# Decode attention over two key/value caches: the small cache and each head of the large one as loop bodies with fixed buffers

## The chip, the core, the metric

The kernel runs on one core of a Trainium2 chip. The metric is device time in microseconds (us). All runs quoted here are fast (granted clock 0.83 to 0.85), and a kernel's time is the median of its runs, unless "span" is said: the span is that of the one profiled execution, which is shorter than the time of the same run.

## The reference, cut to what matters

One token is decoded against two caches. Problem A (the "large cache") has 32 heads with their own keys and values; problem B (the "small cache") has 8 key/value heads, each shared by 4 query heads, and looks at the last 4096 keys only.

```python
# A: x [1,1,512], k_cache and v_cache [1, 32, 32768, 128] bf16, wq [512, 4096], wo [4096, 512]
q = (x @ wq).reshape(B, Sq, 32, 128).transpose(0, 2, 1, 3)
scores = einsum("bhqd,bhkd->bhqk", q, k_cache) * 128 ** -0.5
o = einsum("bhqk,bhkd->bhqd", softmax(scores), v_cache)
out_A = o.transpose(0, 2, 1, 3).reshape(B, Sq, 4096) @ wo
# B: the same with k_cache and v_cache [1, 8, 32768, 128]; k, v = last 4096 keys, each head repeated 4 times
return concatenate([out_A, out_B], axis=-1)
```

One head of A has 8.39 MB of keys and as many values; the used part of B has 8.39 MB of keys and 8.39 MB of values in all. Every byte is used once, so this is a stream from memory with a little arithmetic hung on it.

## The kernel before

Loads are issued by SyncE in program order on one queue, and they come in in that order (the four loads issued in the first 3 us of the trace, 4.19 MB each, have landed at about 13, 24, 34 and 44 us). `kbuf` has three parts ("thirds") of 32 KB per partition, `vbuf` has two. A large head's keys take two thirds, its values all of `vbuf`.

The names in the code: `qproj` is the query projection; `unit` the transposes of a group's or head's keys and the score matmuls; `stats` the maximum and the exponential of the scores; `PT` the transposes of the exponentials and `PV` their product with the values; `spread` what closes a cache. A score matmul is 32 columns wide (`128*32` in the profile's lines, where a transpose has `128*128`); its place, a column strip, is set by `tile_position`, and it writes 32 partitions.

```python
    def load_b(self, which, g):                # small cache: group g (4 heads) has its own third / half
        w = HALF * DH
        dst = {"k": self.kbuf, "v": self.vbuf}[which][:, w * g:w * g + w].rearrange("p (s x) -> p s x", s=4)
        self.load(dst, self.kv_src(which, "B", g), self.mark(which, g), self.free[which][g])
        # kv_src: "s (p j) d -> p s (j d)", p=128: 8 KB runs

    def k_thirds(self, g):
        return (1, 0) if g % 2 == 0 else (1, 2)

    def load_v(self, g):                       # large cache: waits until both halves of vbuf are free
        self.load(self.vbuf[:, :], self.kv_src("v", "A", g)[:, 0, :], self.mark("v", 0), *self.free["v"])

    # plan(), the order of the work
        self.load_wq("B")                      # into half 0 of vbuf
        self.load_b("k", 0)
        self.load_wq("A")                      # into half 1 of vbuf
        self.load_b("k", 1)
        self.emit_qproj("B")
        self.emit_unit("B", 0)
        self.emit_qproj("A")                   # frees half 1 of vbuf
        self.emit_stats("B", 0)
        self.emit_unit("B", 1, {1: lambda: self.emit_PT("B", 0)})
        self.emit_stats("B", 1)
        for g in range(2):
            if g == 1:
                self.emit_PT("B", g)
            self.load_b("v", g)
            self.emit_PV("B", g)
        self.emit_spread("B")
        for g in range(NQH):
            self.loop = {"pe": g // 2, "dve": g // 2}     # two heads per iteration
            self.load_k(g, 1 if g < NQH - 1 else 2)
            self.load_v(g)
            self.emit_qcopy(g)
            self.emit_unit("A", g)             # transposes of the keys and score matmuls
            self.emit_stats("A", g)
            self.emit_PT("A", g)
            self.emit_PV("A", g)

    # a batch: 8 transposes into PSUM, one copy to kt; then the scores, four column strips at a time
    def emit_S(self, key):
        # ... (win: the 32 columns that hold the query in its place)
                for c in range(STRIPS):
                    inst = e.matmul(self.S[32 * c:32 * c + 32, :], lhsT=win,
                                    rhs=self.kt[(bb + c // 2) % NKT][:, 512 * (c % 2):512 * (c % 2) + 512],
                                    start=begin, stop=end, tile_position=(0, 32 * c), skip_group_check=True)
```

Of the kernel before, what the change touches and what calls it, by code (L numbers as in the profile page):

```python
# [35 lines left out]
class Op:  # L36
# [5 lines left out]
    __slots__ = ("eng", "fn", "deps", "loop", "pos", "to", "users", "before")  # L42

    def __init__(self, eng, fn, deps, to, loop):
        self.eng = eng
        self.fn = fn
        self.deps = [d for d in deps if d is not None]
        self.to = to
        self.loop = loop
        self.users = []  # L50


class _Kernel:

    def __init__(self, nc, a, b, out):
# [27 lines left out]
        self.loop = {}  # L83



    def op(self, eng, fn, *deps, to=None):
        o = Op(eng, fn, deps, to, self.loop.get(eng))
        self.prog[eng].append(o)
        return o  # L90
# [15 lines left out]
    def assign(self, eng):  # L106


        ops = self.prog[eng]
        pos, last = 0, None  # L110
        for o in ops:
            pos = pos + 1 if o.loop is not None and o.loop == last else 0
            o.pos, last = pos, o.loop
# [43 lines left out]
    def emit(self, eng):  # L157
        ops = self.prog[eng]
        nit = len({o.loop for o in ops} - {None})
        its = [[o for o in ops if o.loop == k] for k in range(nit)]  # L160
        first = next((i for i, o in enumerate(ops) if o.loop is not None), len(ops))
        pre, post = ops[:first], ops[first + sum(map(len, its)):]
# [17 lines left out]
        def body(e):  # L180
            seen, base = {}, {}
            straight(e, pre, seen, base)
            if not nit:
                return

# [5 lines left out]
            for name in [x for x in sems if not step[x]]:  # L191
                if top(0, name) > seen.get(name, 0):
                    e.wait_ge(sems[name], top(0, name))
                    seen[name] = top(0, name)
                del sems[name]
# [18 lines left out]
            for name, sem in sems.items():  # L214
                if start[name] > 0:
                    e.sem_inc(sem, -start[name])._wait_ge(sem, start[name])
                elif start[name] < 0:
                    e.sem_inc(sem, -start[name])
            with e.Fori(0, nit):
                for o, w in zip(its[-1], plans[-1]):  # L220
                    run(e, o, [(sems[name], rel) for name, rel in w])
                for name, sem in sems.items():
                    e.sem_inc(sem, -step[name])._wait_ge(sem, step[name])
            for name in sems:
                base[name] = seen[name] = start[name] + step[name] * nit
            straight(e, post, seen, base)
# [3 lines left out]
    def alloc(self):  # L230
# [4 lines left out]
        self.kt = [sb(f"kt{i}", [128, 1024], BF16) for i in range(NKT)]  # L235
# [13 lines left out]
        for name, d in self.X.items():  # L249
# [3 lines left out]
                oc=[sb(f"oc_{name}{i}", [128, DH + 1], F32) for i in range(2)],  # L253
# [3 lines left out]
                nb=sb(f"nb_{name}", [128, 2], F32),  # L257
# [9 lines left out]
        self.qa = sb("qa", [128, NQH], BF16)  # L267
        self.qw = sb("qw", [128, 64], BF16)
# [8 lines left out]
        self.ksem = [s(f"ksem{i}") for i in range(2)]  # L277
        self.vsem = [s(f"vsem{i}") for i in range(2)]
# [22 lines left out]
    def load_b(self, which, g):  # L301

        w = HALF * DH
        dst = {"k": self.kbuf, "v": self.vbuf}[which][:, w * g:w * g + w].rearrange("p (s x) -> p s x", s=4)
        self.load(dst, self.kv_src(which, "B", g), self.mark(which, g), self.free[which][g])
# [44 lines left out]
    def plan(self):  # L350
# [12 lines left out]
        self.load_b("k", 0)  # L363
        self.load_wq("A")
        self.load_b("k", 1)
        self.emit_qproj("B")
        self.emit_unit("B", 0)
        self.emit_qproj("A")
        self.emit_stats("B", 0)
        self.emit_unit("B", 1, {1: lambda: self.emit_PT("B", 0)})  # L370
        self.emit_stats("B", 1)
        for g in range(2):
            if g == 1:
                self.emit_PT("B", g)
            self.load_b("v", g)
            self.emit_PV("B", g)
        self.emit_spread("B")

        for g in range(NQH):
            self.loop = {"pe": g // 2, "dve": g // 2}  # L380
            self.load_k(g, 1 if g < NQH - 1 else 2)
            self.load_v(g)
            self.emit_qcopy(g)
            self.emit_unit("A", g)
# [12 lines left out]
    def constants(self):  # L397
# [8 lines left out]
        pool(lambda g: g.memset(self.qw[:, :], 0.0))  # L406
        pool(lambda g: g.memset(self.spread[:, :, :], 0.0))
        pool(lambda g: g.memset(self.rows64[:, :], 0.0))
        pool(lambda g: g.memset(self.nscale[:, :], -self.SCALE))
        for n in ("B", "A"):  # L410
            pool(lambda g, n=n: g.memset(c[n]["hsel"][:, :], 0.0))
# [27 lines left out]
    def emit_qproj(self, name):  # L439
        t = self.c[name]  # L440
        slot = self.WQ_SLOT[name]
        ps, wq = self.ACC, self.vbuf[:, HALF * DH * slot:HALF * DH * (slot + 1)]
        def mm(e):
            inst = None
            for tt in range(4):
                for h in range(NQH):
                    inst = e.matmul(ps[:, h:h + 1], lhsT=wq[:, 4096 * tt + 128 * h:4096 * tt + 128 * h + 128],
                                    rhs=t["x"][:, tt:tt + 1], start=(tt == 0 and h == 0), stop=(tt == 3),
                                    skip_group_check=True)
            return inst  # L450
        o = self.op("pe", mm, (self.xsem[name], 16), self.landed("v", slot), self.accread, to="dve")
        self.free["v"][slot] = o
        if name == "B":
            o = self.op("dve", lambda v: v.tensor_copy(
                self.qz[:, 32:].rearrange("p (k w) -> p k w", w=32)[:, 0:8, 0:4],
                ps[:, 0:NQH].rearrange("p (k a) -> p k a", a=4)), o, self.k_pool)
            self.qb = o
        else:
            o = self.op("dve", lambda v: v.tensor_copy(self.qa[:, :], ps[:, 0:NQH]), o)
            self.qready = o  # L460
        self.accread = o

    def emit_qcopy(self, g):
        self.qcopy = self.op("act", lambda s: s.activation(
            out=self.qw[:, 32:33], in_=self.qa[:, g:g + 1], func=ACTF.Copy), self.qready, self.k_hw, to="pe")

    def emit_unit(self, name, g, hooks={}):

        d = self.X[name]
        thirds = (g,) if name == "B" else self.k_thirds(g)  # L470
        lo = min(thirds)
        order = [(t, i, 8 * (t - lo) + st) for i, t in enumerate(thirds) for st in range(8)]
        for n, (t, i, st) in enumerate(order):
            for half in range(2):
                self.emit_T(HALF * lo + 16 * st + 8 * half, self.landed("k", g if name == "B" else i), t)
            if n % 2:
                if n // 2 in hooks:
                    hooks[n // 2]()
                self.pending.append((name, g, order[n - 1][2], n == 1, n == len(order) - 1, self.nbatch - 4))
                if len(self.pending) > 1:  # L480
                    self.emit_S(self.pending.pop(0))

    def emit_T(self, tile, landed, third):
# [3 lines left out]
        src = self.kbuf[:, DH * tile:DH * tile + 1024]  # L487
        def tr(e):
            inst = None
            for k in range(8):  # L490
                inst = e.transpose(T[:, 128 * k:128 * k + 128], src[:, DH * k:DH * k + DH], self.ident[:, :])  # L491
            return inst
        o = self.op("pe", tr, landed, self.copies[b - NT] if b >= NT else self.k_ident, to="dve")
        self.copies.append(self.op("dve", lambda v: v.tensor_copy(KT[:, :], T[:, :]), o, to="pe"))  # L494
        self.free["k"][third] = o

    def emit_S(self, key):
        name, g, st0, first, last, b0 = key
        d = self.X[name]
        for st in (st0, st0 + 1):  # L500
            s, kc = divmod(st, d["KC"])
            row = kc * d["HG"] + s * d["rep"]
            if name == "A":
                win = self.qw[:, 32 - row:64 - row]
            else:
                off = 32 + 32 * (g * d["kvg"] + s) - row
                win = self.qz[:, off:off + 32]
            bb = b0 + 2 * (st - st0)
            begin, end = first and st == st0, last and st > st0
            def mm(e, win=win, bb=bb, begin=begin, end=end):  # L510
                inst = None
                for c in range(STRIPS):
# [4 lines left out]
            o = self.op("pe", mm, self.qcopy if name == "A" else self.qb, self.copies[bb + 1],  # L517
                        self.sread if first else None, to="dve" if end else None)
        self.sdone = o

    def emit_stats(self, name, g):

        self.emit_S(self.pending.pop(0))
# [3 lines left out]
        k = g % 2  # L527
# [4 lines left out]
        if name == "A":  # L532
# [7 lines left out]
            o = dve(lambda v: v.tensor_copy(t["nb"][:, k:k + 1], self.ACC[:, 64:65]), o, to="act")  # L540
            self.sread = self.op("act", lambda s: s.activation(  # L541
                out=self.psb[:, :], in_=self.S[:, :], func=ACTF.Exp, bias=t["nb"][:, k:k + 1], scale=self.SCALE,
                accum_out=t["oc"][k][:, DH:DH + 1]), o, self.psread, to="pe")
# [5 lines left out]
        for c in range(STRIPS):  # L549
# [4 lines left out]
        o = dve(lambda v: v.tensor_scalar_mul(t["nb"][:, k:k + 1], t["cm"][:, 0:1], -self.SCALE), o, to="act")  # L554
        self.sread = self.op("act", lambda s: s.activation(
            out=self.psb[:, :], in_=self.S[:, :], func=ACTF.Exp, bias=t["nb"][:, k:k + 1], scale=self.SCALE,
            accum_out=t["oc"][k][:, DH:DH + 1]), o, self.psread, to="pe")

    def emit_PT(self, name, g):
        d, t = self.X[name], self.c[name]  # L560
        PT = self.PT[:, :].bitcast(BF16)
        def pt(e):
            inst = None
            for jj in range(4):
                inst = e.transpose(PT[:, 128 * jj:128 * jj + 128], self.psb[:, 128 * jj:128 * jj + 128], self.ident[:, :])  # L565
# [4 lines left out]
        if name == "A":  # L570
            self.hcopy = self.op("act", lambda s: s.activation(
                out=self.hw[:, :], in_=t["hsel"][:, 32 - g:64 - g], func=ACTF.Copy), self.k_sel, to="pe")

    def emit_PV(self, name, g):
# [8 lines left out]
        else:  # L583
            w = HALF * DH
            vv = self.vbuf[:, w * g:w * g + w].rearrange("p (s t x) -> p s t x", s=4, x=DH)
# [10 lines left out]
        pv = self.op("pe", mm, self.landed("v", 0 if name == "A" else g), self.ptread, self.accread, to="sp")  # L596
# [107 lines left out]
```

## Time and profile before

| | before |
|---|---|
| time, median of 4 runs | 1328.89 us (1328.62 to 1329.13) |
| span of the profiled run | 1326.8 us |
| bytes loaded | 570.43 MB, 430 GB/s over the span |
| TensorE waits for large keys | 164.4 us, 31 times |
| first large V load issued | 67.61 us |

From the page of the kernel before: what the DMA engines moved in 40 equal slices of the span, and the load queue (q1) and an instruction queue (q8; the page doesn't name its engine, the author took it as TensorE's, since no other engine has so long a program) with packets, MB and their share of 16 engines.

```profile
GB/s 394 431 431 438 432 433 433 437 429 433 433 435 437 433 435 431 433 433 435 437 433 435 431 433 433 431 441 433 431 435 433 431 433 441 433 431 435 433 431 344
...
q1 hardware_dynamic: 12776, 570.43, 99.6%
q8 instruction: 12, 0.20, 0.1%
```

The row is flat: between the first and the last slice nothing falls under 429 GB/s. The packets of the load queue fill 99.6% of the time of the 16 DMA engines, so this stream is what bounds the kernel.

From the timeline of the kernel before, 54 to 135 us: start, length, engine and line, what, and in brackets how long the engine had been idle and what ended it. SPq is SyncE issuing a load.

```profile
54.63 0.34 SPq L286 DMA_DIRECT2D kbuf<-in_A_k_cache_dram  x1
...
67.61 0.34 SPq L286 DMA_DIRECT2D vbuf<-in_A_v_cache_dram  x1
...
83.45 5.79 PE L491 MATMUL psT<-ident,kbuf 128*128 128x128 bf16 x64 [12.95 <-DMA kbuf<-in_A_k_cache_dram]
...
94.49 0.33 SPq L286 DMA_DIRECT2D kbuf<-in_A_k_cache_dram  x1
...
115.97 0.33 SPq L286 DMA_DIRECT2D vbuf<-in_A_v_cache_dram  x1
```

The first large K load is issued at 54.63 and has landed at 83.45, where TensorE starts on it. The first large V load was issued at 67.61, so it stood in the queue 16 us before its turn.

From the windows of the kernel before: each stretch with its length, the busy time of PE (TensorE's matmuls), its weight loads, DVE, ACT and POOL, the granted clock, the DMA share and, in the last column, GB/s. Over a few us the last two are rough, and shares above 1 occur.

```profile
42.00:46.00 4.00, 1.84 (x18) 1.84 (x19) 1.86 (x8) 0.78 (x2) 0.00 (x0) 0.50 1.00 412
...
80.00:86.00 6.00, 2.55 (x25) 2.55 (x26) 1.31 (x2) 0.00 (x0) 0.00 (x0) 0.50 0.98 426
86.00:90.00 4.00, 4.00 (x55) 3.47 (x54) 3.52 (x7) 0.00 (x0) 0.00 (x0) 0.78 0.95 410
90.00:96.00 6.00, 6.00 (x104) 4.95 (x101) 6.00 (x11) 0.00 (x0) 0.00 (x0) 1.00 1.18 505
```

### The profile page before, as it was taken

What the parts mean: (1) busy time and instruction counts of PE and PEld (TensorE: products, weight loads), DVE (VectorE), ACT (ScalarE), POOL (GpSimd) and SP (SyncE); (2) the same over time, 40 slices, a digit from 0 to 9 for tenths busy, and PEclk for the clock granted to TensorE, in tenths of its full rate; (3) what the DMA queues carried; (4) which work ended last, traced back from release to release, by engine and by line L of the source; (5) the groups of instructions that cost most, each with busy time, mean ns of one, the idle gap of its engine ahead of it and who ended that gap; (6) DMA issues with size and microseconds to landing.
All of it is one profiled execution on the core that took longest, in us unless ns stands there. A gap on an engine that the chain in (4) does not pass through costs nothing.

```text
span 1326.8 us, 28797 instructions
## 1 busy us (share of the span) xinstructions
PE 964.5 (73%) x13436; PEld 679.5 (51%) x13436; DVE 749.8 (57%) x1345; ACT 54.8 (4%) x167; POOL 2.3 (0%) x17
## 2 busy tenths in 40 slices
PE   3757678777667877766787777678777767877786
PEld 3544455554445555444565544456554445655453
DVE  3645466665456666545666645566654556665473
ACT  0000000000000000000000000000000000000000
POOL 0000000000000000000000000000000000000000
PEclk9877788887788888778888878888887888888798
DMA  9999999999999999999999999999999999999998
GB/s 394 431 431 438 432 433 433 437 429 433 433 435 437 433 435 431 433 433 435 437 433 435 431 433 433 431 441 433 431 435 433 431 433 441 433 431 435 433 431 344
DMA packets 13079, 570.66 MB, mean 430 GB/s; under 512 B 1540, under 2 KB 1544, under 8 KB 1928
## 3 DMA queue, kind: packets, MB, share of 16 engines
q1 hardware_dynamic: 12776, 570.43, 99.6%
q8 instruction: 12, 0.20, 0.1%
q10 hardware_dynamic: 288, 0.00, 0.0%
q14 instruction: 3, 0.02, 0.0%
HBM read 570.43 MB, written 0.00 MB: 430 GB/s over the span
## 4 chain that ended last, share of the span: by engine, by line
DMA 70%; PE 28%; DVE 1%; issue 0%; SPq 0%; ACT 0%
DMA kbuf<-in_A_k_cache_dram 65%; PE psT L491 23%; PE psS L513 4%; DMA kbuf<-in_B_k_cache_dram 3%; DMA kbuf<-in_A_wo_dram 3%; DVE kt L494 1%; PE psACC L593 0%; SPq L286 0%; DVE oc_A L609 0%; ACT psb L541 0%; DVE tr_in L530 0%; PE psPT L565 0%; ACT ptsb L568 0%; PE psPT L655 0%; PE psG L620 0%
## 5 line engine op out<-in xcount | busy, mean ns | idle before, releaser
L494 DVE COPY kt<-psT 128x1024 bf16<-128x1024 bf16 x1056 | 655.2, 684 | 245.0 <-PE psT L491 243.1
L491 PE MATMUL psT<-ident,kbuf 128*128 128x128 bf16 x8448 | 579.2, 234 | 176.2 <-DMA kbuf<-in_A_k_cache_dram 164.4
L491 PEld LDWEIGHTS psT<-ident,kbuf 128*128 128x128 bf16 x8448 | 539.7, 106 | 268.2 <-DMA kbuf<-in_A_k_cache_dram 172.5
L593 PE MATMUL psACC<-vbuf,ptsb 128*4 128x512 bf16 (+1 forms) x2112 | 183.2, 523 | 23.1 <-ACT ptsb L568 21.3
L513 PE MATMUL psS<-kt,qw 128*32 128x512 bf16 x2048 | 157.6, 385 | 15.5 <-DVE kt L494 15.5
L607 DVE TENSOR_SCALAR oc_A<-psACC,hot_A 128x128 f32<-128x128 f32 x32 | 11.2, 351 | 247.8 <-PE psG L620 247.8
L593 PEld LDWEIGHTS psACC<-vbuf,ptsb 128*4 128x4 bf16 (+1 forms) x2112 | 60.0, 110 | 136.9 <-issue 87.2
L541 ACT ACTIVATE psb<-psS,nb_A 128x512 bf16<-128x512 f32 x32 | 22.0, 687 | 1169.9 <-DVE nb_A L540 1169.9
L513 PEld LDWEIGHTS psS<-kt,qw 128*32 128x32 bf16 x2048 | 34.0, 95 | 58.0 <-DVE kt L494 31.4
L620 PE MATMUL psG<-oc_A,hw 128*32 128x128 f32 (+1 forms) x128 | 19.3, 227 | 52.3 <-DVE oc_A L609 52.3
L620 PEld LDWEIGHTS psG<-oc_A,hw 128*32 128x32 f32 x128 | 11.4, 109 | 62.4 <-DVE oc_A L609 55.0
L565 PE MATMUL psPT<-ident,psb 128*128 128x128 bf16 x136 | 17.9, 274 | 34.0 <-ACT psb L541 34.0
L609 DVE SCALAR_TENSOR_TENSOR oc_A<-psACC,hot_A,oc_A 128x128 f32<-128x128 f32 x96 | 33.7, 351 | 3.4
L530 DVE TENSOR_REDUCE tr_in<-psS 128x1 f32<-128x512 f32 x34 | 23.5, 692 | 17.1 <-PE psS L513 17.1
L565 PEld LDWEIGHTS psPT<-ident,psb 128*128 128x128 bf16 x136 | 10.0, 116 | 37.0 <-ACT psb L541 36.7
L534 PE MATMUL psACC<-rows,tr_in 128*1 128x64 f32 x64 | 8.7, 217 | 25.6 <-DVE tr_in L530 25.6
L568 ACT ACTIVATE ptsb<-psPT 128x512 bf16<-128x512 bf16 x34 | 20.3, 597 | 28.2 <-PE psPT L565 28.2
L534 PEld LDWEIGHTS psACC<-rows,tr_in 128*1 128x1 f32 x64 | 2.7, 81 | 35.1 <-DVE tr_in L530 35.1
L538 PE MATMUL psACC<-mr_A,nscale 1*128 1x1 f32 x64 | 12.1, 256 | 9.8 <-DVE mr_A L537 9.8
L538 PEld LDWEIGHTS psACC<-mr_A,nscale 1*128 1x128 f32 x64 | 9.4, 183 | 15.7 <-DVE mr_A L537 15.7
L540 DVE COPY nb_A<-psACC 128x1 f32<-128x1 f32 x32 | 5.1, 158 | 15.0 <-PE psACC L538 15.0
L537 DVE TENSOR_REDUCE mr_A<-psACC 1x1 f32<-1x64 f32 x32 | 6.8, 213 | 11.7 <-PE psACC L534 11.7
(71 smaller groups left out, 75.1 us busy)
## 6 DMA issues: line engine op xcount, KB each, us to landing
kbuf<-in_B_k_cache_dram SPq DMA_DIRECT2D x2, 4096.0 KB, 32.5
vbuf<-in_B_v_cache_dram SPq DMA_DIRECT2D x2, 4096.0 KB, 23.6
kbuf<-in_A_k_cache_dram SPq DMA_DIRECT2D x2, 4096.0 KB, 22.0
vbuf<-in_B_wq_dram SPq DMA_DIRECT2D x1, 4096.0 KB, 12.3
vbuf<-in_A_wq_dram SPq DMA_DIRECT2D x1, 4096.0 KB, 32.4
kbuf<-in_B_wo_dram SPq DMA_DIRECT2D x2, 2048.0 KB, 33.1
kbuf<-in_A_wo_dram SPq DMA_DIRECT2D x1, 1408.0 KB, 28.5
kbuf<-in_A_wo_dram SPq DMA_DIRECT2D x1, 1024.0 KB, 30.6
```

The source lines that it names most:

```text
L491: inst = e.transpose(T[:, 128 * k:128 * k + 128], src[:, DH * k:DH * k + DH], self.ident[:, :])
L494: self.copies.append(self.op("dve", lambda v: v.tensor_copy(KT[:, :], T[:, :]), o, to="pe"))
L513: inst = e.matmul(self.S[32 * c:32 * c + 32, :], lhsT=win, rhs=self.kt[(bb + c // 2) % NKT][:, 512 * (c % 2):512 * (c % 2) + 512], start=b ...
L530: o = dve(lambda v: v.reduce_max(tr["in"][:, 0:1], self.S[:, :], axis=AXX), self.sdone, self.k_pool, to="pe" if name == "A" else None)
L534: o = self.op("pe", lambda e: e.matmul(self.ACC[0:1, 0:64], lhsT=tr["in"][:, 0:1], rhs=self.rows64[:, :], start=True, stop=True, skip_grou ...
L538: o = self.op("pe", lambda e: e.matmul(self.ACC[:, 64:65], lhsT=self.nscale[:, :], rhs=t["mr"][0:1, :], start=True, stop=True, skip_group_ ...
L541: self.sread = self.op("act", lambda s: s.activation(out=self.psb[:, :], in_=self.S[:, :], func=ACTF.Exp, bias=t["nb"][:, k:k + 1], scale= ...
L565: inst = e.transpose(PT[:, 128 * jj:128 * jj + 128], self.psb[:, 128 * jj:128 * jj + 128], self.ident[:, :])
L568: self.ptread = self.op("act", lambda s: s.activation(out=self.ptsb[:, :], in_=PT[:, 0:512], func=ACTF.Copy), self.psread, to="pe")
L593: inst = e.matmul(acc[32 * c:32 * c + rows, 0:512], lhsT=lhsT, rhs=rhs, start=begin, stop=end, tile_position=(0, 32 * c), skip_group_check ...
L609: o = self.op("dve", lambda v, src=src, hot=hot: v.scalar_tensor_tensor(out=oc, in0=src, scalar=hot, in1=oc, op0=ALU.mult, op1=ALU.add), p ...
L620: return self.op("pe", lambda e: e.matmul(self.G[0:32, c0 + c:c0 + c2], lhsT=win, rhs=t["oc"][g % 2][:, c:c2], start=False, stop=True, ski ...
```

## The change

Its intent is a smaller program. The small cache becomes a TensorE loop over two groups of heads, and the large cache a loop over single heads instead of pairs; for this the buffers are fixed, so that each pass uses the same addresses. Where the two passes of a pair differ, an if/else picks the side. The small cache's keys are loaded in 32 KB runs: each of the 128 partitions holds 128 neighbouring keys of one head (partition 4b+s: block b, head s). After the transposes the four heads are interleaved, so a score matmul for one head has to pick its columns out of the transposed keys. The core of the diff, with cuts:

```diff
+        kt = [sb(f"kt{i}", [128, 2048], BF16) for i in range(NKT // 2)]
+        self.ktp = [x[:, :].rearrange("p (m i b s) -> p m b i s", m=4, i=4, s=4) for x in kt]
 ...
+    def load_bk(self, g):
+        d = self.X["B"]
+        src = d["k"][0, 4 * g:4 * g + 4, d["key0"]:d["key0"] + d["NKEYS"], :].rearrange("s (b j) d -> b s (j d)", b=32)
         w = HALF * DH
+        self.load(self.kbuf[:, 2 * w:3 * w], src, self.kbsem, self.free["k"][2])
 ...
         self.load_wq("B")
-        self.load_b("k", 0)
+        self.load_bk(0)
         self.load_wq("A")
-        self.load_b("k", 1)
         self.emit_qproj("B")
-        self.emit_unit("B", 0)
+        self.load_bv(0)
+        for g in range(2):
+            self.loop = {"pe": ("b", g)}
+            self.emit_qcopy("B", g)
+            self.emit_unit_b(g)
+            self.emit_stats("B", g)
+            self.emit_PT("B", g)
+            self.emit_PV("B", g)
+            if g == 0:
+                self.load_bk(1)
+                self.load_bv(1)
+        self.loop = {}
+        self.emit_spread("B")
         self.emit_qproj("A")
 ...
         for g in range(NQH):
-            self.loop = {"pe": g // 2, "dve": g // 2}
+            self.loop = {"pe": ("a", g), "dve": ("a", g)}
 ...
+    def emit_Sb(self, step, b0):
+            for s in range(4):
+                for x in range(2):
+                    kc, c = divmod(2 * step + x, 4)
+                    row = 16 * kc + 4 * s
+                    inst = e.matmul(self.S[32 * c:32 * c + 32, :], lhsT=self.qzw[:, 32 + 32 * s - row:64 + 32 * s - row],
+                                    rhs=self.ktp[(b0 // 2 + x) % (NKT // 2)][:, :, :, :, s], start=(kc == 0 and s == 0),
+                                    stop=(kc == 1 and s == 3), tile_position=(0, 32 * c), skip_group_check=True)
 ...
+                        with e.If_eq(odd, 0):          # second half of a large head: its third is 0 or 2
+                            for o, _, w in ops:
+                                run(e, o, [(sems[name], rel) for name, rel in w])
+                        with e.Else():
```

The query projection is also rewritten: rows of 512 on four column strips, then turned, instead of 128 matmuls with one column each. The projection for the large cache now comes after the small cache.

## The prediction

> **What bounds the kernel now.** The DMA engines. The page counts 570.43 MB on the load queue in a span of 1326.8 us, 430 GB/s, and 429 to 441 GB/s in every slice but the first and last (394, 344). The chain of waits gives DMA 70%, PE 28%; PE stands there where a load was issued early and queued behind another. In the timeline the large cache's key loads are issued every 38.2 us (94.49, 132.65); 16.78 MB (one head's K and V) at 433 GB/s take 38.7 us: the queue never runs dry. PE needs 34.6 us for head 0 (83.45 to 118.0); the waits view shows it idle for keys 164.4 us over 31 heads, 5.3 us each. So compute has 4 to 5 us of slack per head, and only DMA idle time or DMA rate moves the span.
>
> **What the change does, costed.**
> 1. Bytes: the same. The small cache's keys (8.4 MB) go from 8 KB to 32 KB runs. The windows show about 418 GB/s from 32 to 56 us, where 8 KB runs flow, against 433 later: 20.1 against 19.4 us, a gain of 0.7 us on the DMA chain.
> 2. The small cache is serialised: both key groups share one buffer. The second key load waits for the first group's transposes (done near 39 us); wq_A and the first V load keep the queue fed to 44 us, so no gap. Its keys land near 53.5 instead of 44.1 us, and the second PV ends near 75 instead of 67.6 us.
> 3. The query projection of the large cache moves from 36 us to behind the small cache. It frees the half of the value buffer that the first large V load needs. From the old durations (S to exp 3.4 us, exp to PV 5, PV to spread 6.4, then about 3.5 for a projection at the lower clock there) I put that load's issue near 82 us, against 67.6. The first large K load, issued near 49, lands near 82.8. [...] a hole of 1 to 4 us opens in the DMA stream near 82 us and is never regained: estimate +2.5 us.
> 4. Large-cache loop: one head per iteration on PE and DVE, with an if/else for the second half of the transposes. [...] In this trace the PE loop ran 16 times while its instruction queue (q8) moved 12 packets, 0.20 MB: the body was not refetched. The new body is shorter, so I expect under 1 us per head, hidden by the key wait. First passes may stall some us once.
> 5. Single oc and nb buffers: reused a head later; no wait.
>
> **Sum.** 1328.7 - 0.7 + 2.5: 1330.5 us, range 1326.5 to 1337. Faster by over 2%: 1%; within 2%: 95%; slower: 4%.
>
> **What would show the steps.** Windows: 430 GB/s or more in the middle slices, one dip near 80 to 86 us. DMA: fewer packets (by about 768). Waits: SP's wait for the first large V load ends on the projection near 82 us. PE's key wait stays over 3 us per head, q8 near 12 packets.
>
> **What would make it wrong.** If branches and back edge cost over 5 us per head [...], PE becomes the bound and each further us per head costs 32 us. If the projection frees the value buffer before 80 us there is no hole, and the time falls slightly below before.

"The lower clock there" is a granted clock of 0.56, 0.59 and 0.84 in the windows 60 to 64, 64 to 68 and 68 to 72 us of the kernel before, and the stall that step 4 allows a first pass was 3.42 us, once, in the change.

## More of the kernel before

The program is recorded as a list of operations per engine with their dependencies, and then emitted; an operation signals one other engine when it is done.

Matmuls on different strips overlapped: in the kernel before, eight on four strips took 0.61 us, where one took 0.38.

From the view of one tile, the score tile `psS`, 20 to 60 us: durations in ns, least, median and most, of the small cache's 64 score matmuls.

```profile
L513 PE MATMUL psS<-kt,qz x64: 378/384/391, 30.6 to 55.5; 128*32 128x512 bf16 x64
```

## The result, and the profile after

| | before | after |
|---|---|---|
| time, median of 4 runs | 1328.89 us | 1343.42 us (1341.05 to 1344.27) |
| span of the profiled run | 1326.8 us | 1341.1 us |
| bytes loaded, GB/s over the span | 570.43 MB, 430 | 570.43 MB, 425 |
| TensorE waits for large keys | 164.4 us, 31 times | 146.0 us, 30 times |
| first large V load issued | 67.61 us | 95.26 us |

The ratio is 1.0106, with a 95% interval of 1.0093 to 1.0119. Ratios here are the mean time of one kernel's fast runs over that of the other's of the same rounds, so they are not quite the ratio of the medians. The change is slower by 14.5 us, inside the 2% band and outside the predicted range.

From the page after: the DMA rate by slices, and the two queues.

```profile
GB/s 394 341 329 432 438 434 418 438 434 434 438 436 434 420 438 436 430 438 436 436 424 434 438 430 436 436 436 426 432 438 430 436 434 436 430 430 438 432 434 354
...
q1 hardware_dynamic: 12008, 570.43, 98.6%
q8 instruction: 7, 0.11, 0.0%
```

The whole loss stands in two of 40 slices, the second and the third, 33 to 101 us. From there on the rate is that of before. The two slices lack some 90 and 102 GB/s against 431; a slice is 33.5 us, so (90 + 102) / 431 x 33.5 = 14.9 us. That is the difference.

From the timeline after, 28 to 108 us.

```profile
29.02 3.72 PE L535 MATMUL psS<-kt,qzw 128*32 128x512 bf16 x8
...
45.43 0.58 SPq L309 DMA_DIRECT2D kbuf<-in_B_k_cache_dram  x1
...
55.73 0.51 SPq L309 DMA_DIRECT2D kbuf<-in_A_k_cache_dram  x1
...
58.72 5.26 PE L564 MATMUL psT<-ident,kbuf 128*128 128x128 bf16 x64 [1.38 <-DMA kbuf<-in_B_k_cache_dram]
...
95.26 0.34 SPq L309 DMA_DIRECT2D vbuf<-in_A_v_cache_dram  x1
...
96.31 5.22 PE L564 MATMUL psT<-ident,kbuf 128*128 128x128 bf16 x64 [0.22 <-PEq L212]
```

The windows after, the same stretches.

```profile
42.00:46.00 4.00, 4.00 (x16) 0.51 (x12) 0.43 (x1) 0.00 (x0) 0.00 (x0) 1.00 0.02 8
...
80.00:86.00 6.00, 1.13 (x14) 0.53 (x16) 2.99 (x13) 1.60 (x5) 0.00 (x0) 0.70 1.08 470
86.00:90.00 4.00, 3.17 (x34) 1.18 (x26) 0.71 (x3) 0.00 (x0) 0.00 (x0) 0.60 0.04 16
90.00:96.00 6.00, 4.00 (x46) 1.66 (x46) 2.76 (x7) 0.00 (x0) 0.00 (x0) 0.72 0.01 3
```

There are two holes in the stream: one of about 4 us from 42 us, and one of about 10 us from 86 us, which ends with the issue of the first large V load. Between them they hold most of the loss. And the score tile after, 20 to 82 us:

```profile
L535 PE MATMUL psS<-kt,qzw x64: 1052/1061/1137, 29.0 to 79.0; 128*32 128x512 bf16 x64
```

The small cache's score matmuls take 1061 ns each instead of 384, and a block of eight takes 3.72 us. No term of the prediction has these matmuls at a new duration. TensorE, which had time to spare in this stage before, is now busy from 23 us to 46 us with the first group alone.

From the waits of SyncE (the DMA queue's own), 0 to 100 us: what it waited for, us in total, times, longest.

```profile
SPq L309 <- PE psS L496: 53.9, 2, 38.9
SPq L309 <- PE psS L535: 27.4, 1, 27.4
```

L496 is the projection, L535 are the slow matmuls. The V load was released by the projection, as predicted, but 13 us later than predicted. The second small key load (45.43) was released by a score matmul and not by the last transposes, which were over at 41.71 us: in this program an operation signals only one other engine, and the transposes signal VectorE.

### The profile page after: what moved, and what is told of

Same layout as the page of the kernel before. It is cut to its first block, busy times and chain, and to the rows that moved or that the text cites. A ratio compares the mean times of both kernels' runs of the same rounds, so it can differ in the third digit from the quotient of the medians.

```text
span 1341.1 us, 28761 instructions
## 1 busy us (share of the span) xinstructions
PE 991.8 (74%) x13260; PEld 682.9 (51%) x13260; DVE 754.1 (56%) x1349; ACT 56.2 (4%) x173; POOL 2.6 (0%) x20
## 3 DMA queue, kind: packets, MB, share of 16 engines
q1 hardware_dynamic: 12008, 570.43, 98.6%
HBM read 570.43 MB, written 0.00 MB: 425 GB/s over the span
## 5 line engine op out<-in xcount | busy, mean ns | idle before, releaser
L564 PE MATMUL psT<-ident,kbuf 128*128 128x128 bf16 x8448 | 584.1, 235 | 153.1 <-DMA kbuf<-in_A_k_cache_dram 146.0
L662 PE MATMUL psACC<-vbuf,ptsb 128*4 128x512 bf16 (+1 forms) x2112 | 186.1, 529 | 23.4 <-ACT ptsb L637 23.4
L535 PE MATMUL psS<-kt,qzw 128*32 128x512 bf16 x64 | 24.6, 1068 | 0.0
L637 ACT ACTIVATE ptsb<-psPT 128x512 bf16<-128x512 bf16 x34 | 20.3, 597 | 21.3 <-PE psPT L634 21.3
```

The costliest lines, as they stand in the source:

```text
L535: inst = e.matmul(self.S[32 * c:32 * c + 32, :], lhsT=self.qzw[:, 32 + 32 * s - row:64 + 32 * s - row], rhs=self.ktp[(b0 // 2 + x) % (NKT ...
L564: inst = e.transpose(T[:, 128 * k:128 * k + 128], self.kbuf[:, DH * tile:DH * tile + DH], self.ident[:, :])
L637: self.ptread = self.op("act", lambda s: s.activation(out=self.ptsb[:, :], in_=PT[:, 0:512], func=ACTF.Copy), self.psread, to="pe")
L662: inst = e.matmul(acc[32 * c:32 * c + rows, 0:512], lhsT=lhsT, rhs=rhs, start=begin, stop=end, tile_position=(0, 32 * c), skip_group_check ...
```

## The experiments

The theory: the score matmuls are slow because they read the transposed keys at a step of 256 bytes (the index `i` runs fastest in `ktp`, and its step is 128 elements of 2 bytes). They lengthen the chain from the second small key load to the end of the small cache; the first large V load hangs on that end; until it is issued the queue has nothing more to do. The rivals: the loop and its branches (L); the shared key buffer and the late projection, whatever the matmuls cost (B); the number of column strips, two instead of four; a loss in the first hole by itself.

The first four runs shared one chip and one set of runs of the kernel before (1328.98 us).

### s8: the step from 256 to 8 bytes

```diff
-        self.ktp = [x[:, :].rearrange("p (m i b s) -> p m b i s", m=4, i=4, s=4) for x in kt]
+        self.ktp = [x[:, :].rearrange("p (m i b s) -> p m i b s", m=4, i=4, s=4) for x in kt]
 ...     # small cache only: the exponential puts its columns back into the order that V has
-                out=self.psb[:, :], in_=self.S[:, :], func=ACTF.Exp, ...
+                out=self.psb[:, :].rearrange("p (m b i) -> p m i b", m=4, i=4), in_=self.S[:, :], func=ACTF.Exp, ...
```

> The changed kernel with one thing different: the small cache's score matmuls read the transposed keys at a step of 4 elements (8 bytes) instead of 128 elements (256 bytes); the exponential writes its columns back into the old order, so the result stays right. Theory S (the far-apart reads slow these matmuls, which delays the end of the small cache and with it the first large V load): a block of 8 score matmuls falls from 3.7 us to about 0.9 us, the second small key load is issued near 38.5 us instead of 45.4, the first large V load near 80 us instead of 95.3, and the time falls to 1328 to 1330.5 us. Rival B (shared buffer and late projection alone, whatever the matmuls cost): the V load stays after 88 us, time above 1336. Rival L (loop and branch of the large cache): no change, 1341 to 1344.

Measured: 1333.83 us (1333.78 to 1334.45), ratio to before 1.0038. 9.6 of the 14.5 us are gone with one index order. From the tile view and the timeline of this run:

```profile
L535 PE MATMUL psS<-kt,qzw x64: 608/629/632, 28.2 to 69.2; 128*32 128x512 bf16 x64
```

```profile
28.23 1.97 PE L535 MATMUL psS<-kt,qzw 128*32 128x512 bf16 x8
...
37.81 0.58 SPq L309 DMA_DIRECT2D kbuf<-in_B_k_cache_dram  x1
...
86.47 0.34 SPq L309 DMA_DIRECT2D vbuf<-in_A_v_cache_dram  x1
```

The expectation was too hopeful: the 8 byte step was not free (629 ns for one matmul, against 379 in the next run). A block takes 1.97 us, not 0.9, and the V load comes at 86.47, not 80. The direction holds and rival L falls; the rest of the loss is larger than expected. A small part of that rest is the repair: the exponential that writes its columns back into order took 1392 ns, against 688 in the change.

### contig: contiguous reads, wrong result

```diff
-                                    rhs=self.ktp[(b0 // 2 + x) % (NKT // 2)][:, :, :, :, s], ...
+                                    rhs=self.kt[(b0 + 2 * x + s // 2) % NKT][:, 512 * (s % 2):512 * (s % 2) + 512], ...
```

> Wrong result on purpose: the small cache's score matmuls read contiguous 512 element pieces. Theory S: as the run with the 8 byte step within 0.5 us if 8 bytes is near enough to be free; if any step costs, this one is faster than that one and a block of 8 takes visibly less. Rival L: no change, 1341 to 1344.

Measured: 1330.66 us (1330.27 to 1331.33), ratio 1.0012 (0.9996 to 1.0029).

```profile
L535 PE MATMUL psS<-kt,qzw x64: 379/379/390, 29.3 to 67.6; 128*32 128x512 bf16 x64
```

A block takes 1.04 us, and the V load is issued at 83.19 us. So the three steps give 379, 629 and 1061 ns for one matmul. In a block of eight on two strips four follow one another, so the block less one record, divided by three, gives an estimate of what one costs when they follow closely: (1.04 - 0.38) / 3 = 0.22 us, (1.97 - 0.63) / 3 = 0.45 us, (3.72 - 1.06) / 3 = 0.89 us. By it the 8 byte step doubled the cost and the 256 byte step made it four times as long; no run shows why a step costs. The step is not all of it: the run bstride below also reads at 256 bytes, but eight elements before it jumps back where the change reads four, and one matmul takes 1284 ns there. No run separates the step from the length of these runs.

With contiguous reads the changed kernel is 1.7 us above before by the medians (the interval allows no difference), close to the +1.8 of the prediction's sum. That closeness is partly luck: the sum has a gain of 0.7 us for the longer runs, which no time shows, and this run still has two strips, on which a contiguous block takes 1.04 us instead of 0.6. But the bulk of what the prediction left out, 12.8 of 14.5 us, goes with the pattern of this read.

This run and the other ones that mix up keys passed the comparison with the reference. So the comparison doesn't see the order of keys, presumably because scores this small make a nearly flat softmax; that the run with 8 bytes is right rests on its index order, not on the comparison.

### strips4: the 256 byte step on four strips, wrong result

```diff
-                    inst = e.matmul(self.S[32 * c:32 * c + 32, :], ...
-                                    ... start=(kc == 0 and s == 0), stop=(kc == 1 and s == 3), tile_position=(0, 32 * c), ...
+                    inst = e.matmul(self.S[32 * s:32 * s + 32, :], ...
+                                    ... start=(step == 0 and x == 0), stop=(step == 3 and x == 1), tile_position=(0, 32 * s), ...
```

> Wrong result on purpose: the 256 byte step stays, but the score matmuls go round four column strips instead of two. If the far-apart reads are slow for each stream by itself, four streams overlap and a block of 8 falls from 3.7 to about 1.9 us, the time to about 1332. If the streams share the reading, or if only two strips were ever the reason, this tells: shared reading leaves 3.7 us and 1341 to 1344 us; were two strips instead of four the whole cause, a block would fall to the 0.6 us of the kernel before and the time to 1329.

Measured: 1334.44 us (1334.29 to 1334.89), ratio 1.0042. From its tile view and its timeline:

```profile
L535 PE MATMUL psS<-kt,qzw x64: 1041/1061/1277, 28.6 to 69.7; 128*32 128x512 bf16 x64
```

```profile
28.57 1.98 PE L535 MATMUL psS<-kt,qzw 128*32 128x512 bf16 x8
```

One matmul is as slow as in the change (1061 ns), but four at once take about the time of one (eight on four strips 1.98 us): the slowness belongs to each stream, and these streams overlapped. Two strips instead of four thus nearly doubled the block, from 1.98 to 3.72 us. Both halves of the story are the layout's doing: with the new layout a step of the loop fills only two strips. The block came out as expected; the time stayed 2.4 us above what was expected.

### unroll2: the large cache's loop put back

```diff
-            self.loop = {"pe": ("a", g), "dve": ("a", g)}
+            self.loop = {"pe": ("a", g // 2), "dve": ("a", g // 2)}
 ...
-            self.alt = i == 1
+            self.alt = False
 ...     # the same for the last block of scores
-        self.alt = name == "A"
+        self.alt = False
```

> The changed kernel with the loop of the large cache put back to two heads per iteration and no if/else. Theory S: no change, 1341 to 1344 us, first large V load still near 95 us. Rival L (back edges and branches cost the time): the 14 us come back, 1329.

Measured: 1343.61 us (1343.08 to 1344.05), ratio 1.0110, and the V load at 95.66 us. Rival L falls: neither the branch nor twice as many back edges cost any time that can be seen. The traces show one stall, though. In the first large head of the change, TensorE sits idle 3.42 us before the matmul behind the maximum, and the profile shows nothing that it waits for; in later heads, before the change and here it is 0.80 us, the wait for VectorE. In the kernels that keep both this branch and the small cache's loop the stall is 3.4 to 7.3 us, once; the run unshare, which keeps the branch and unrolls the small loop, has none. With an uncut V load it costs no time: the run contig, with the longest, lies on the same line as the others (last table). The prediction's reading of q8 held: it moved 12 packets, 0.20 MB, over 16 passes before and 7 packets, 0.11 MB, over 32 passes after, fewer packets than passes.

The next four runs shared a chip with runs of the kernel before at 1328.87 us.

### k8: the 32 KB runs alone undone

```diff
-        src = ....rearrange("s (b j) d -> b s (j d)", b=32)
-        self.load(self.kbuf[:, 2 * w:3 * w], src, self.kbsem, self.free["k"][2])
+        src = ....rearrange("s (p j) d -> p s (j d)", p=128)
+        self.load(self.kbuf[:, 2 * w:3 * w].rearrange("p (s x) -> p s x", s=4), src, self.kbsem, self.free["k"][2])
 ...     # transposes of tiles in order, then per head and half the old four strips
+                for c in range(STRIPS):
+                    inst = e.matmul(self.S[32 * c:32 * c + 32, :], lhsT=self.qzw[:, 32 + 32 * s - row:64 + 32 * s - row],
+                                    rhs=self.kt[(b0 + 2 * (st % 2) + c // 2) % NKT][:, 512 * (c % 2):512 * (c % 2) + 512], ...
```

> The changed kernel with the 32 KB runs alone undone: 8 KB runs, contiguous reads and four strips as before; shared key buffer, loops and late projection stay. Theory S: first large V load issued near 82 to 83.5 us, time 1330 to 1331.3 us, so that all but about 2 us of the loss goes with this part. If shared buffer and late projection alone made the loss: 1336 or more.

Measured: 1329.65 us (1329.00 to 1329.89), ratio 1.0006 (0.9991 to 1.0021); one matmul 384 ns, V load at 81.45 us. The load came a little earlier than expected, and the time is a little below its range. The loops, the fixed buffers and the late projection together cost 0.8 us by the medians, which the interval doesn't tell from nothing. Rival B in its plain form falls: they are harmless (0.8 us here) unless TensorE is slow in this stage.

### bstride: the slow reads alone, put into the kernel before, wrong result

```diff
+                    kt = self.kt[(bb + c // 2) % NKT]
+                    rhs = kt[:, 512 * (c % 2):512 * (c % 2) + 512]
+                    if name == "B":
+                        rhs = kt[:, :].rearrange("p (i b) -> p b i", i=8)[:, 64 * (c % 2):64 * (c % 2) + 64, :]
```

> Wrong result on purpose: the kernel before, with its small cache's score matmuls reading at a 256 byte step, nothing else changed. Theory S with its condition (slow matmuls cost only where the first large V load hangs on them late): each matmul goes from 384 to about 1060 ns, the first large V load moves from 67.6 to 71 to 75 us, which is before the 80.6 us to which the runs so far extrapolate, so the time stays at 1328.7 to 1329.3. Rival: slow matmuls cost time by themselves, 1334 or more.

Measured: 1330.13 us (1329.99 to 1330.67), ratio 1.0009 (0.9993 to 1.0024); one matmul 1284 ns, V load at 77.29 us. A miss in each number: the matmul is slower than the 1060 ns expected, the V load later than 71 to 75 us, and the time 1.3 us above before where at most 0.4 was expected (the interval still allows no difference).

```profile
L517 PE MATMUL psS<-kt,qz x64: 1247/1284/1318, 30.3 to 65.3; 128*32 128x512 bf16 x64
```

The trace shows where the time goes. The first large K load waits for the second small group's transposes and is issued at 63.32 instead of 54.63 us, and the window at that place has a small hole:

```profile
62.00:64.00 2.00, 2.00 (x9) 0.25 (x12) 1.24 (x3) 0.00 (x0) 0.00 (x0) 1.00 0.19 78
```

The blocks here are not those of the change: on four strips eight of these matmuls take 2.42 us, not 3.72. The run with a similar block in the new order is strips4 (1.98 us). So slow matmuls on four strips cost 1.3 us in the old order, the new order without them costs 0.8 us (k8), and both together cost 5.5 us (strips4), and 14.5 us with two strips. The loss is not a sum of parts: each part eats slack, and only together do they eat more than there is.

### early: the second small key load released sooner

```diff
+            if step == 3:       # an empty matmul behind the last transpose, to signal SyncE
+                self.op("pe", lambda e: e.matmul(self.G[0:1, 500:501], lhsT=self.ident[:, 0:1], rhs=self.ident[:, 0:1],
+                                                 start=False, stop=True, skip_group_check=True), to="sp")
```

> The changed kernel with an empty matmul behind the last transpose of a group, so that the second small key load is released some 3.7 us earlier (41.7 instead of 45.4 us). The hole of 42 to 47 us closes. But the second group's transposes can start only when TensorE is through with the first group, 57.4 instead of 58.7 us: the time falls by about 1.4 us, to 1340 to 1342.5. Were the first hole a loss of its own, 4 us would come back: 1339 or less.

Measured: 1341.83 us (1341.72 to 1341.94), ratio 1.0097, beside runs of before at 1329.01. The load is issued at 39.60 us, nearly 6 us earlier than in the change, and the V load at 94.14 us, 1.1 us earlier. A hole moves from 42 to 52 us, in front of the next load. The first hole is no loss of its own: what is late is the end of the chain.

### unshare: two key buffers for the small cache, both loaded at the start

```diff
+        t = 2 * g
+        self.load(self.kbuf[:, w * t:w * t + w], src, self.ksemb[g])
 ...
         self.load_wq("A")
+        self.load_bk(1)
         self.emit_qproj("B")
 ...
-            self.loop = {"pe": ("b", g)}
```

> The changed kernel with two key buffers for the small cache, both loaded at the start, and its loop unrolled; slow matmuls and late projection stay. If the slow matmuls rule (TensorE busy from 23 to 57 us with the first group, then the second at once): first large V load near 93.9 us, 1339.5 to 1342.5. If the shared buffer is what costs: 1332 or less.

Measured: 1342.24 us (1342.01 to 1343.58), ratio 1.0099. So the shared buffer isn't what costs: with both keys loaded early, TensorE comes to the second group at 59.45 us, later even than in the change (58.72). The V load came at 95.91 us, 2 us later than expected. The timeline shows why: the first group's values now queue behind the second keys, and their product waits for them.

```profile
53.64 3.59 PE L662 MATMUL psACC<-vbuf,ptsb 128*16 128x512 bf16 x32 [2.76 <-DMA vbuf<-in_B_v_cache_dram]
```

In the change that product waits 0.69 us. Without the other 2.1 us the second group could have started near 57.4 us, so by this estimate the shared buffer costs 1.3 us of the 14.5; that is about what the change waits for its second keys (1.38 us, line at 58.72).

### vsplit and s8vs: the first large V load cut in two

```diff
+        if g == 0:
+            w = HALF * DH
+            for i in (0, 1):
+                self.load(self.vbuf[:, w * i:w * i + w], src[:, w * i:w * i + w], self.mark("v", i), self.free["v"][i])
+        else:
             self.load(self.vbuf[:, :], src, self.mark("v", 0), *self.free["v"])
+            sem = self.mark("v", 1)
+            self.op("sp", lambda e: e.sem_inc(sem, 16))
```

> The changed kernel with its first large V load cut in two: the half whose buffer the small cache's values leave is issued when the second PV ends, near 89.3 us, the other after the projection near 95.3 us. The slow matmuls stay. If the loss is the hole in the DMA stream before that load, it shrinks by the 6 us between the two: 1336 to 1338 us. If the loss lies elsewhere: 1341 to 1344.

> The 8 byte step and the cut V load together, right result: first half issued near 80.3 us, second near 86.5. The hole is gone or under 1 us: 1328 to 1329.5 us, equal to the kernel before or up to 0.9 us better.

Measured: with the slow matmuls 1340.63 us (1340.37 to 1342.44), ratio 1.0087; with the 8 byte step 1332.64 us (1330.38 to 1334.51), ratio 1.0033. Both missed: some 3 us came back where 6 were expected, and in the second 1 us where 4 to 5 were. The timeline of the first of them, and two of its windows:

```profile
90.51 7.25 SPq L309 DMA_DIRECT2D vbuf<-in_A_v_cache_dram  x2
...
98.67 5.44 PE L572 MATMUL psT<-ident,kbuf 128*128 128x128 bf16 x64 [0.40 <-PEq L212]
...
123.84 0.37 PE L610 MATMUL psACC<-rows,tr_in 128*1 128x64 f32 x2 [3.46 <-issue]
...
133.86 0.33 SPq L309 DMA_DIRECT2D vbuf<-in_A_v_cache_dram  x1
```

```profile
126.00:130.00 4.00, 3.15 (x32) 1.17 (x36) 0.00 (x0) 0.92 (x5) 0.00 (x0) 0.50 1.08 463
130.00:134.00 4.00, 3.84 (x46) 1.39 (x38) 0.09 (x1) 0.00 (x0) 0.00 (x0) 0.62 0.12 49
```

The hole came back one head later. TensorE starts on the first large head at 98.67 us, against 83.45 before. There is one value buffer, so the second V load waits for that head's PV; it is issued at 133.86, when the queue had run dry at about 130. Feeding the queue sooner doesn't make the late engine early. Part of that lateness is the stall of the first pass: 3.46 us before the line at 123.84, where later heads wait 0.80. It is 2.7 us of chain, and this hole is about 3.5 us long; in the run with the 8 byte step the stall is 5.43 us, and the queue runs low there too (180 GB/s from 118 to 122 us, the second V load at 121.66). So with the cut V load the stall stands where it can cost time; a run without it was not made. The profiled run with the slow matmuls is the slowest of its four (1342.44; the others 1340.37 to 1340.75). Why the runs with the 8 byte step and the cut load differ among themselves by 4 us stays open; the profiled one is the fastest (span 1328.6).

### k8vs and contigvs: nothing late

> Right result: 8 KB runs with contiguous reads, and the cut V load. The cut V load gained only about 3 of 6 us with slow matmuls, because head 0's transposes then start 15 us later than before and the second large V load waits for head 0's PV. Here head 0 starts near 83.5 us as before and the first half of V is issued before 78 us: no hole, 1328.2 to 1329.2 us. If cutting the V load itself costs (two queues' worth of issue, extra semaphore), it is slower than the uncut run's 1329.65.

> Wrong result on purpose: 32 KB runs, contiguous reads, cut V load. Head 0 starts near 84 us, no hole: 1327.8 to 1329.2 us. Against the 8 KB runs with the cut V load this is what the longer runs are worth by themselves: the prediction said 0.7 us; if they are worth nothing, the two agree within 0.3 us.

These are the same cut of the V load on top of the 8 KB run and of the contiguous run. Measured beside runs of before at 1329.01: 8 KB runs 1327.92 us (1327.13 to 1329.43), ratio 0.9995 (0.9981 to 1.0008); 32 KB runs with the wrong result 1329.98 us (1327.76 to 1331.18), ratio 1.0004 (0.9990 to 1.0017). The first keeps the loops and fixed buffers of the change and is as fast as the kernel before. That it beats it is not shown, since the interval holds 1. Both times miss their expected ranges, the first by 0.3 us below and the second by 0.8 us above. The timeline of the first has the order of before again:

```profile
74.53 6.91 SPq L309 DMA_DIRECT2D vbuf<-in_A_v_cache_dram  x2
...
83.27 5.37 PE L572 MATMUL psT<-ident,kbuf 128*128 128x128 bf16 x64 [1.30 <-DMA kbuf<-in_A_k_cache_dram]
```

The 32 KB runs are worth nothing that the times show, and the two kernels don't agree within 0.3 us either: the one with 32 KB runs is 2.1 us slower. They also differ in their strips, and the runs of each spread over 2.3 and 3.4 us, so their times say less than the landings. The first small keys are ready for the transposes at 23.18 us with 8 KB runs and at 23.07 with 32 KB, the second at 53.98 and 53.80; in the pair with the uncut V load, k8 and contig, it is 23.27 and 23.23, then 54.37 and 53.64. A gain of 0.1 to 0.7 us on the way to the second keys is thus possible, and none is shown in the time.

### What the runs say together

For every kernel with an uncut V load and the late projection, the issue of the first large V load and the span of the profiled run:

| kernel | V load issued, us | span, us | span less issue |
|---|---|---|---|
| k8 | 81.45 | 1327.3 | 1245.9 |
| contig | 83.19 | 1329.2 | 1246.0 |
| s8 | 86.47 | 1332.1 | 1245.6 |
| strips4 | 86.79 | 1332.7 | 1245.9 |
| early | 94.14 | 1340.1 | 1246.0 |
| the change | 95.26 | 1341.1 | 1245.8 |
| unroll2 | 95.66 | 1341.4 | 1245.7 |
| unshare | 95.91 | 1341.9 | 1246.0 |

The last column is constant to 0.4 us over a spread of 14.6 us. After that load everything takes the same 1246 us, and the time is set by when it is issued. The kernel before, at 67.61, is off this line (1259.2), because there the load waited in the queue; 1326.8 - 1245.9 = 80.9 us is, by this line, the moment up to which lateness of this load is free. (In bstride it came at 77.29, and the 1.3 us were lost at the K load before it.)

## Why the prediction was wrong, point by point

- **The bound.** Right. The DMA engines bound the kernel (99.6% of their time filled before, 98.6% after), and the change lost its time where they had nothing to do. The loss stands in two slices of the rate.
- **Step 1, "a gain of 0.7 us on the DMA chain".** Not shown. The packets fell by 768 as predicted, from 12776 to 12008, but the second small keys land only 0.2 or 0.7 us earlier, depending on the pair of runs, and no time shows it.
- **Step 2, "done near 39 us" and "so no gap".** Wrong: the second small key load was issued at 45.43 us, and from 42 to 46 us the stream moved 8 GB/s. The cause is that of step 3: with contiguous reads it was issued at 36.12 us and the same stretch moved 430 GB/s. The run with the early release shows that this hole is not a loss by itself.
- **Step 3, "from the old durations ... I put that load's issue near 82 us".** This is the step that failed. The mechanism was right: a hole in front of the first large V load, released by the projection and never regained. Its size was wrong: 95.26 instead of 82 us, because the chain was put together from old durations, and that of the score matmuls no longer held. They have no term of their own; they sit in the time from a group's first transposes to its last score matmul, which was 11.7 us for the second group before (44.16 to 55.89) and is 21.3 us after (58.72 to 80.06). The change gives them a new read pattern, 256 byte steps on two strips, and a block took 3.72 instead of the 0.6 us of before. With contiguous reads the load comes at 83.19 and the time is 1330.66 us, where the sum said 1330.5 (in part by luck, as said there). Against that run the slow reads cost 12.1 us of the chain: 5.1 in the first group (its successor starts at 58.72 instead of 53.64 us) and 7.0 in the second.
- **Step 4, the loop.** Right. The kernel without the branch and with the old loop takes the same time (1343.61 us against 1343.42), and the instruction queue moved less than before (0.11 MB against 0.20). Why the branch is cheap no run shows. "First passes may stall some us once" was seen too: 3.42 us in the first large head, off the path that sets the time.
- **Step 5, single buffers.** Right as far as k8 shows, which keeps them and is 0.8 us above before.
- **What would make it wrong.** It named branches and an early projection. It didn't ask whether an instruction with a new access pattern still has its old duration.

## What to carry to other kernels

When a layout is changed for the sake of a load, follow it to every later reader: each access pattern that becomes new needs its own cost, since a duration taken from the old trace need not hold for it: here 384 ns became 1061 ns. In a kernel bound by one queue, find the first load that depends on finished compute and note how long it stands in the queue; here that margin was some 13 us (80.9 less 67.61). Slow matmuls by themselves used 9.7 of it (V load at 77.29), the new order by itself all of it (81.45), with no more than 1.3 us showing in the time; together, and on two strips, they overran it by 14 us. And a buffer freed sooner helps only as far as the engine that fills the next wait is in time, as the cut V load showed (its hole came back at 130 us).
